# Spreading the rounding of weight blocks over the steps, and loading two inputs at once

## The chip, the cores and the metric

The kernel runs on one core of a Trainium2 chip. Its engines work side by side, each through its own queue of instructions: TensorE (PE in the profile) multiplies matrices, VectorE (DVE), ScalarE (ACT) and GpSimd (POOL) work elementwise, and SyncE (SP) issues transfers; ScalarE and GpSimd issue some too. The metric is the device time of one execution in microseconds (us), as the median of the runs; lower is better.

## The reference

A batch of 8 sequences of 3008 tokens with 256 channels is filtered in the frequency domain, and a two-layer network with SiLU between its layers follows, token by token:

```python
X = np.fft.rfft(x, axis=1)
Y = X * (filt_r + 1j * filt_i)[None]
y = np.fft.irfft(Y, n=3008, axis=1).reshape(24064, 256)
h = y @ w_in                     # 256 -> 2048
out = (h / (1 + np.exp(-h))) @ w_out   # 2048 -> 256
```

The weights w_in and w_out arrive as 64-bit numbers and are turned into 32-bit ones inside the kernel, on their bits.

## The kernel before, in words

**Two halves that overlap.** The Fourier part of a batch (`spectral(b)`) is a chain of small matmuls with fixed tables: `stage1` over blocks of rows, `forward`, a product with the filter, `inverse`, and `stage3`, which leaves the batch as y. The network part runs over pairs (batch, half, range of tokens), 48 of them, in steps: each pair takes 8 steps, and step jp of a pair uses the weights of hidden units 256 jp to 256 jp + 255. The first batch's Fourier part has nothing to run beside and comes first, with as much of the weights as fits; from then on the steps run without a break, and the Fourier part of the next batch is put between their matmuls.

**A step** is written as two generators. `hidden(step)` (lines 737 to 784) multiplies by the first layer with seven matmuls in place of eight (a Strassen-like scheme with combined weights), `project(step)` (line 796) multiplies the step before by the second layer, seven matmuls again. Each step has 8 rounds; in each round one piece of `hidden` is written, one piece of `project`, and then all pieces that were put there by `put(step, round, piece)` and are due. The order in which the code writes them is the order in each engine's queue. In `hidden` the matmuls and sums, by the names used from here on, are:

- round 0: matmul A11 into the bank px; ScalarE copies it (first copy).
- round 1: matmul A12 into one half of the bank pyz; VectorE makes *sum 1* of it and the first copy; then the *late pair*, the two last differences of the step before (`finish`).
- round 2: matmul S2 on px; second copy; SiLU of sum 1.
- round 3: matmul S1 into the other half of pyz.
- round 4: matmul S3 on px; third copy; *sum 2* of S1 and the third copy.
- round 6: matmul A22 on px; SiLU straight from px, which frees it for the next A11; SiLU of sum 2.
- round 7: matmul S4 on the S1 half; *sum 3* of it and the second copy; SiLU of sum 3; then the *differences* of three results (one instruction of 512 columns).

The matmul S1 waits for sum 1 and A12 of the next step for sum 3. In steps 1 to 6 the second batch's `stage1` (two matmuls of 512 columns, line 335) comes after round 3.

**Weight blocks.** There are 16 blocks of 128 hidden units, j = 0 to 15. Step jp of a pair needs blocks 2 jp and 2 jp + 1. A block is loaded (`weights`), split into exponent and mantissa (`split`: two VectorE instructions at lines 945 and 947, then two on ScalarE at 952 and 953), rounded (`rounded`: three VectorE instructions at 965, 967, 971), and put in its places (`placed`: two at 980). For each pair of blocks four combinations follow (`combine_weights`, line 721 of the helper `combine`), in one go or in two halves. Blocks 0 to 8 are done before the steps begin, blocks 9 to 15 inside steps 0 to 6 by the `put` calls at lines 1170 to 1182, each split, rounded (and, for the first three, with the four combinations of an earlier pair between) in round 1 and placed in round 5.

**The time before the steps.** The second batch's first two inputs are loaded by GpSimd's queue (line 1115) into the two halves of `x_all`, which the first batch used until its last first-stage matmul; two pairs of `stage1` matmuls of the second batch (line 1143) read them. Their results are stored to DRAM by GpSimd (`store_rows`), behind a small copy into `gate` (line 1151) that makes the stores wait for a block to be placed. Dummy matmuls (`idle_wide`, line 1154) fill TensorE's wait for the last transposed data of the first batch; then come four `stage3` and the steps.

Of the kernel before, what the change touches and what calls it, by code (L numbers as in the profile page):

```python
# [58 lines left out]
NJ = DFF // 128  # L59
# [8 lines left out]
A11, A12, S3, A22, S1, S2, S4 = range(7)  # L68
ROUNDS = 8
# [101 lines left out]
def kernel(  # L171
# [9 lines left out]
    nc = tc.nc  # L181
# [46 lines left out]
    w_t = cpool.tile([128, NJP, 7, 2, 128], FP32)  # L228
    warm = cpool.tile([128, 1], FP32)
    bias_t = cpool.tile([128, 5], FP32)  # L230
    gate = cpool.tile([128, 1], FP32)
    x_all = xpool.tile([128, 2, 2, 2 * C], FP32)
    x_t = [x_all[:, i] for i in range(2)]
# [34 lines left out]
    def spectral(b):  # L268
# [4 lines left out]
        xs, us, t2s, banks, prods, halves, t4s = {}, {}, {}, {}, {}, {}, {}  # L273
# [33 lines left out]
        def load_x(u, queue=None):  # L307
# [6 lines left out]
            for h in range(2):  # L314
                for r0, nr in ((0, 32), (32, N1 - 32)):
# [3 lines left out]
                                    offset=x.offset + (b * S + 32 * r0 + 4 * u + 2 * h) * C,  # L319
                                    ap=[[32 * C, nr], [32 * N1 * C, 2], [1, 2 * C]]))  # L320

        def sums(u):
            ut = x_t[0] if u == 7 else upool.tile([128, 2, 512], FP32, name=f"u_{b}_{u}", tag="u")
            xt = xs.pop(u)
            for par, op in ((0, ALU.add), (1, ALU.subtract)):
                nc.vector.tensor_tensor(out=ut[0:111, par], in0=xt[0:111, 0], in1=xt[0:111, 1], op=op)
            us[u] = ut
# [268 lines left out]
        def evict_y(g, h):  # L596
# [2 lines left out]
            copy = nc.scalar.copy if h else nc.vector.tensor_copy  # L599
            copy(out=dst[:, :, h, :, n0:n0 + 4], in_=us["pd", g][h].rearrange("p a i n -> p a n i"))  # L600

        return dict(us=us, store_rows=store_rows, evict_y=evict_y, evict_t1=evict_t1, halves=halves, load_first=load_first, stage1_first=stage1_first, load_x=load_x, sums=sums, stage1=stage1, reverse_x=reverse_x,
                    load_fold=load_fold, fold=fold, stage1_fold=stage1_fold, evict_fold=evict_fold,
                    load_t2=load_t2, forward=forward, multiply=multiply, add=add, inverse=inverse, inverse_first=inverse_first, rows_first=rows_first, even=even, rows=rows, load_t4=load_t4, load_t4_rows=load_t4_rows, stage3=stage3)

# [5 lines left out]
    def put(step, rnd, piece, *args):  # L611

        pending.append((step + rnd / ROUNDS, len(pending), lambda: piece(*args)))
# [103 lines left out]
    v, gp = nc.vector, nc.gpsimd  # L717
    ty, g_t, acc, unfinished = {}, {}, {}, []

    def combine(eng, out, in0, in1, op):  # L720
        eng.tensor_tensor(out=out, in0=in0, in1=in1, op=op)  # L721
# [176 lines left out]
    def load_weights(j, queue=None):  # L898

        if j in (8, 11, 12, 13):  # L900
            pool, tag = (t4pool, "t4") if j in (11, 12) else (upool, "u")
            raw = pool.tile([128, 2, 512], U32, name=f"raw_{j}", tag=tag)
        else:

            if j in (0, 2):
                t = ypool.tile([128, 2, HALF], FP32, name=f"raw_{j}", tag="y")
                raws.setdefault("tiles", []).append(t)
                raws["at"] = t.rearrange("p a n -> p (a n)").bitcast(U32)[:, 0:2048]
                raws["y"] = raws["at"]
                raws.setdefault("first", raws["at"])  # L910
            elif j == 4:
                raws["at"] = spool.tile([128, 2048], U32, name=f"raw_{j}", tag="s")
            elif j == 6:
                raws["at"] = gpool.tile([128, 2048], U32, name=f"raw_{j}", tag="g")
            elif j in (9, 14):
                raws["at"] = raws["y"]
            at = 1024 * (j in (1, 3, 5, 7, 10, 15))
            raw = raws["at"][:, at:at + 1024].rearrange("p (w n) -> p w n", w=2)
        queue = queue or nc.sync
        queue.dma_start(  # L920
            out=raw[:, 0].rearrange("p (a n) -> p a n", a=2),
            in_=moe_w_in.bitcast(U32)[:, 256 * j:256 * j + 256].rearrange("(a p) n -> p a n", p=128))
        queue.dma_start(out=raw[:, 1], in_=moe_w_out.bitcast(U32)[128 * j:128 * j + 128, :])
        raws[j] = raw
# [37 lines left out]
    def round_weights(*js):  # L962
        for j in js:
            lo, hi, e, m, ef, mf, mo, _, _ = raws[j]
            v.scalar_tensor_tensor(out=mo, in0=lo, scalar=2.0 ** -52, in1=mf, op0=ALU.mult, op1=ALU.add)
            if j not in (0, 2, 6):
                v.tensor_scalar(out=e, in0=ef, scalar1=255.0, scalar2=float(1 << 23),
                                op0=ALU.min, op1=ALU.mult)
        for j in js[::-1]:
            hi, e, eo = raws[j][1], raws[j][2], raws[j][8]  # L970
            v.scalar_tensor_tensor(out=eo, in0=hi, scalar=0x80000000, in1=e,
                                   op0=ALU.bitwise_and, op1=ALU.bitwise_or)

    def place_weights(*js, eng=None):
        for j in js:
            mo, eo = raws.pop(j)[6:8]
            for w in range(2):
                cols = slice(256 * w, 256 * w + 256)
                dst = places(j, w) if w == 0 else places(j, w).rearrange("p k (q i) -> p k q i", q=4)
                (eng or v).tensor_tensor(out=dst, in0=columns(mo[:, cols], w), in1=columns(eo[:, cols], w),  # L980
                                         op=ALU.mult)

    def load_exact(j):
        for k in range(2):
            nc.sync.dma_start(out=places(j, 0)[:, k],
                              in_=moe_w_in[128 * k:128 * k + 128, 128 * j:128 * j + 128])
            nc.sync.dma_start(out=places(j, 1)[:, k].rearrange("p (q i) -> p q i", q=4),
                              in_=columns(moe_w_out[128 * j:128 * j + 128, :], 1)[:, k])

    def combine_weights(jp, part=None, eng=None):  # L990

        eng = eng or v

        def w(c):
            return w_t[:, jp, c]
        if part != 1:
            combine(eng, w(S1), w(S3), w(A22), ALU.add)
            combine(eng, w(S2), w(S1), w(A11), ALU.subtract)
        if part != 0:
            combine(eng, w(S3), w(A11), w(S3), ALU.subtract)  # L1000
            combine(eng, w(S4), w(A12), w(S2), ALU.subtract)

    def weights(*js, queue=None):
        for j in js:
            if wide:
                load_weights(j, queue)

    def bits(*js):
        if wide:
            bits_of_weights(*js)  # L1010

    def converted(*js):
        if wide:
            convert_weights(*js)

    def split(*js):
        bits(*js)
        converted(*js)

    def rounded(*js):  # L1020
        if wide:
            round_weights(*js)

    def placed(*js, eng=None):
        if wide:
            place_weights(*js, eng=eng)
        else:
            for j in js:
                load_exact(j)
# [15 lines left out]
    def idle_wide(n, ps=None, rhs=None):  # L1045

        ps = ps or bank(0, "idle")
        for _ in range(n):
            nc.tensor.matmul(out=ps[:, 0], lhsT=wx_t, rhs=wide_rows if rhs is None else rhs,
                             start=True, stop=True)  # L1050
# [3 lines left out]

    by_gpsimd = (0, 1, 2, 3, 4)
    part, second = spectral(0), spectral(1)
    weights(0, 1, 2, 3)
    place = part["load_first"]()
# [35 lines left out]
    for k in range(16):  # L1094
        part["stage1_first"](k, 1)
        if k < 12:
            part["stage1_first"](k + 4, 0)
    weights(6, 7)
    part["forward"](0, fill=4)
    placed(0, 1)  # L1100
# [3 lines left out]
    def products(g):  # L1104
        for k in range(2):
            part["multiply"](g, k)
            if g in by_gpsimd:
                part["add"](g, k)
# [2 lines left out]
        part["inverse_first"](g)  # L1111
        part["rows_first"](g)

    for u in range(2):
        second["load_x"](u, nc.gpsimd)
    products(0)
    products(1)
    inverse(0)
# [26 lines left out]
    placed(4, 5)  # L1145
    rounded(6, 7)
    placed(6, 7)
    split(8)
    rounded(8)
    placed(8)  # L1150
    gp.tensor_copy(out=gate, in_=w_t[:, 4, A11, 0, 0:1])
    for u in range(2):
        second["store_rows"](u)
    idle_wide(14)
    for g in range(4):
        part["stage3"](g)
    nc.sync.dma_start(out=wi_t, in_=wi_dram.ap())
    second["load_x"](2)
    weights(10, 11, 12)
    second["load_x"](3)  # L1160
    weights(13)
    early[0] = None
    plan_rest(0, part)
    for g in (4, 5):
# [2 lines left out]
        put(20, 0, lambda t=t, dram=dram: nc.sync.dma_start(out=t, in_=dram.ap()))  # L1167
    for b in range(1, B):
        plan(b, second if b == 1 else spectral(b))
    for j in range(9, NJ):  # L1170
        if j < 12:
            put(j - 9, 1, lambda j=j: (split(j), combine_weights(j - 8), rounded(j)))
        else:
            put(j - 9, 1, lambda j=j: (split(j), rounded(j)))
        put(j - 9, 5, placed, j)
        if j % 2:

            put(*((j - 8, 5) if j < 15 else (j - 9, 6)), combine_weights, j // 2, 0)
            put(*{13: (j - 8, 7), 15: (j - 8, 1)}.get(j, (j - 7, 5)), combine_weights, j // 2, 1)

        if j < 11:
            put(j - 9, 1, weights, j + 5)

    per = len(PAIRS) * 2

# [4 lines left out]
    for pair in range(len(pairs)):  # L1190
        step, rnd = combines[pair % per] if pair != 1 else (7, 5)
        pending.append((pair // per * STEPS + step + rnd / ROUNDS, 98, lambda pair=pair: tokens(pair)))
        for chunk in range(2 if pair < len(pairs) - 1 else 0):
            step, rnd = stores[pair % per][chunk]
# [56 lines left out]
```

## Time and profile before

| what | value |
|---|---|
| median of 3 runs | 2580.62 us (2579.96 to 2583.24) |
| profiled execution, its own time | 2580.55 us |
| its span in the profile | 2578.7 us |
| TensorE busy | 2555.9 us, 99% |
| VectorE, ScalarE, GpSimd busy | 65%, 42%, 16% |
| dummy matmuls before stage 3 | 62.5 to 68.7 us |
| stage 3 of the first batch | 71.3 to 78.1 us |
| first matmul (A11) of steps 0 to 4 | 78.87, 86.65, 95.48, 103.60, 111.71 us |
| first matmul of steps 5 to 8 | 119.69, 127.54, 136.19, 142.56 us |

All times in the views are microseconds from the start of the span. A row of the timeline gives start, duration, engine, line of the code, operation, and destination and source with their shapes; in brackets stands how long the engine was idle before it and what it waited for. A duration can be longer than the distance to the next start, since an engine takes up the next instruction before the last one has ended. A row of the table of stretches gives the busy time of TensorE, its weight loads, VectorE, ScalarE and GpSimd in that stretch, with the number of instructions, then the granted TensorE clock as a share of full speed, the mean busy share of the transfer engines and GB/s. In the page's row PEclk each digit stands for a fortieth of the span.

### The profile page before, as it was taken

The numbers are of one execution on the slowest core, as the hardware profiler recorded it, in microseconds if no ns is written. First come the engines' busy times: TensorE is split into PE (matmuls) and PEld (weight loads), VectorE is DVE, ScalarE is ACT, GpSimd is POOL, SyncE is SP. The second block draws the span as 40 slices with busy tenths as digits, with TensorE's granted clock in tenths as the row PEclk, the third lists the DMA queues.
The fourth block names the chain that finished last, engine by engine and source line by source line (L and its number), as shares of the span: only waits on it lengthen the run. The fifth ranks groups of instructions, "written<-read, shape, count | busy, mean of one in ns | idle before, by whom it ended". The sixth has DMA issues, their size and how long they took to land.

```text
span 2578.7 us, 48117 instructions
## 1 busy us (share of the span) xinstructions
PE 2555.9 (99%) x18852; PEld 2196.2 (85%) x18852; DVE 1665.8 (65%) x3588; ACT 1086.0 (42%) x3010; POOL 421.3 (16%) x670
## 2 busy tenths in 40 slices
PE   8999999999999999999999999999999999999998
PEld 6788888888888888888888888988888888888987
DVE  7866666666666666666666666666666666555554
ACT  3544444444444444434444434444444444444443
POOL 2211111121112111311122111211121112101101
PEclk9899999999999999999999999999999999999999
DMA  8621232222222222222223222331232311210011
GB/s 277 171 62 50 71 79 63 60 64 75 60 63 69 70 62 58 76 73 64 64 59 88 51 66 58 80 80 46 66 79 65 74 42 28 64 19 16 9 17 16
DMA packets 200443, 171.08 MB, mean 66 GB/s; under 512 B 122100, under 2 KB 174180, under 8 KB 199428
## 3 DMA queue, kind: packets, MB, share of 16 engines
q1 hardware_dynamic: 179000, 117.32, 19.8%
q0 software_dynamic: 16992, 44.91, 5.5%
q10 hardware_dynamic: 4224, 5.77, 0.8%
q8 instruction: 148, 2.42, 0.4%
q14 instruction: 79, 0.65, 0.1%
HBM read 96.07 MB, written 81.26 MB: 69 GB/s over the span
## 4 chain that ended last, share of the span: by engine, by line
PE 97%; DVE 1%; DMA 1%; ACT 0%; issue 0%; SPq 0%; DVEq 0%; ACTq 0%
PE acc L813 44%; PE px L750 26%; PE pyz L750 19%; PE pd L580 3%; PE pb L457 2%; PE pc L500 2%; PE pf L424 1%; PE pc L522 0%; PE pa L344 0%; PE pa L335 0%; DMA d<-q 0%; DMA t<-d 0%; DMA raw<-in_moe_w_in_dram 0%; DVE g L721 0%; DVE w_t L721 0%
## 5 line engine op out<-in xcount | busy, mean ns | idle before, releaser
L813 PE MATMUL acc<-g,w_t 128*128 128x256 f32 (+1 forms) x5376 | 1509.2, 375 | 0.4 <-DVE g L721 0.4
L813 PEld LDWEIGHTS acc<-g,w_t 128*128 128x128 f32 x5376 | 1021.6, 190 | 115.8 <-DVE g L721 0.8
L721 DVE TENSOR_TENSOR g<-pyz,abc 128x256 f32<-128x256 f32 (+1 forms) x1152 | 479.9, 417 | 620.3 <-ACT abc L771 356.0
L721 DVE TENSOR_TENSOR g<-g 128x256 f32<-128x256 f32 (+3 forms) x1152 | 599.4, 520 | 196.7 <-ACT g L754 183.6
L750 PE MATMUL px<-ty,w_t 128*128 128x256 f32 (+1 forms) x2304 | 678.3, 376 | 1.4 <-ACT abc L765 1.0
L754 ACT ACTIVATE g<-g 128x256 f32<-128x256 f32 (+1 forms) x1152 | 472.9, 411 | 250.9 <-DVE g L721 250.9
L750 PEld LDWEIGHTS px<-ty,w_t 128*128 128x128 f32 x2304 | 432.3, 190 | 64.9 <-issue 6.2
L721 POOL TENSOR_TENSOR s<-s 128x256 f32<-128x256 f32 (+1 forms) x329 | 254.8, 792 | 1416.6 <-DVE s L833 1350.6
L750 PE MATMUL pyz<-y,w_t 128*128 128x256 f32 (+1 forms) x1536 | 454.3, 378 | 0.4 <-DVE g L721 0.4
L750 PEld LDWEIGHTS pyz<-y,w_t 128*128 128x128 f32 x1536 | 283.9, 190 | 48.2 <-DVE g L721 7.9
L765 ACT COPY abc<-px 128x256 f32<-128x256 f32 (+1 forms) x384 | 141.3, 368 | 372.8 <-PE px L750 372.8
L771 ACT COPY abc<-px 128x256 f32<-128x256 f32 (+1 forms) x384 | 141.5, 368 | 338.1 <-PE px L750 337.1
L754 ACT ACTIVATE g<-px 128x256 f32<-128x256 f32 (+1 forms) x384 | 145.8, 380 | 300.2 <-PE px L750 300.1
L750 PE MATMUL px<-y,w_t 128*128 128x256 f32 (+1 forms) x768 | 232.7, 385 | 0.8 <-DVE y L594 0.8
L750 PE MATMUL pyz<-ty,w_t 128*128 128x256 f32 (+1 forms) x768 | 225.4, 375 | 0.2 <-DVE g L721 0.2
L750 PEld LDWEIGHTS px<-y,w_t 128*128 128x128 f32 x768 | 140.6, 190 | 32.9 <-DVE y L600 5.8
L750 PEld LDWEIGHTS pyz<-ty,w_t 128*128 128x128 f32 x768 | 144.6, 190 | 18.7 <-DVE g L721 1.0
L758 ACT COPY abc<-px 128x256 f32<-128x256 f32 (+1 forms) x384 | 135.3, 352 | 53.7 <-PE px L750 53.6
L580 PEld LDWEIGHTS pd<-wi_t,t 48*64 48x64 f32 x3840 | 61.3, 135 | 26.2 <-ACT g L754 16.4
L436 POOL DMA_DIRECT2D d<-tf x144 | 71.4, 503 | 30.7 <-DVE tf L432 26.7
L863 DVE STREAM_TRANSPOSE o<-s 128x256 f32<-128x256 f32 x192 | 73.9, 423 | 1.5 <-issue 0.7
L833 ACT COPY s<-acc 128x512 f32<-128x512 f32 (+1 forms) x94 | 54.2, 577 | 47.6 <-PE acc L813 47.5
(137 smaller groups left out, 1262.4 us busy)
## 6 DMA issues: line engine op xcount, KB each, us to landing
t<-d SPq DMA_DIRECT2D x120, 192.0 KB
t<-d SPq DMA_DIRECT2D x84, 256.0 KB
d<-q POOLq DMA_DIRECT2D x84, 256.0 KB, 2.6
out_dram<-o SPq DMA_DIRECT2D x636, 32.0 KB
d<-tf POOLq DMA_DIRECT2D x144, 96.0 KB, 3.3
xr<-in_x_dram SPq DMA_DIRECT2D x6, 1472.0 KB
x_all<-in_x_dram SPq DMA_DIRECT2D x72, 96.0 KB
x_all<-xr SPq DMA_DIRECT2D x72, 96.0 KB
```

What stands on the lines that cost most here:

```text
L436: nc.gpsimd.dma_start(out=d1[k // 2, :, k % 2, n0:n0 + 4], in_=us["tf"][32 * k:32 * k + NS].rearrange("p q n c -> p (q n) c"))
L457: nc.tensor.matmul(out=ps[k][32 * j:32 * j + 32, ri, :], lhsT=d_t[rows, 4 * g + at, ri, :], rhs=rhs, start=True, stop=True)
L580: nc.tensor.matmul(out=ps[h][c0:c0 + 64, cb, i, :], lhsT=t4[rows, i, 128 * cb + c0:128 * cb + c0 + 64], rhs=wi_t[rows, :], start=True, sto ...
L721: eng.tensor_tensor(out=out, in0=in0, in1=in1, op=op)
L750: nc.tensor.matmul(out=out, lhsT=w_t[:, jp, c, 0], rhs=rhs, start=start, stop=True, skip_group_check=True)
L754: nc.scalar.activation(out=g[:, k, 0:n], in_=g[:, k, 0:n] if src is None else src, func=AFT.Silu)
L758: nc.scalar.copy(out=sums[:, 0, 0:n], in_=xo)
L765: nc.scalar.copy(out=sums[:, 1, 0:n], in_=xo)
L771: nc.scalar.copy(out=sums[:, 2, 0:n], in_=xo)
L813: nc.tensor.matmul(out=acc[pair][i][:, h, 0:n], lhsT=w_t[:, jp, c, 1], rhs=g[:, k, 0:n], start=(jp == 0 and h == 0), stop=last, skip_group ...
L833: copy(out=s[:, 2 * i:2 * i + 2, 0:n], in_=acc[pair][i][:, :, 0:n])
L863: v.transpose(out=o[:, :, h, :], in_=results[pair][:, ((2, 6), (4, 1))[chunk][h], :])
```

## The change

The two loads of the second batch's inputs on GpSimd become one on SP, in pieces of 8 KB per row, written between the loads of blocks 5 and 6. Block 8 is no longer split, rounded and placed before the steps: it takes step 0, round 1, and the blocks after it follow at about seven rounds from each other, with the rounding one round after the splitting from block 11 on. The combinations and the loads of blocks 13 to 15 move with them. The gate reads a place of block 6 in place of one of block 8, and there are 16 dummy matmuls instead of 14.

```diff
+        def load_two():
+            load_rows(x_all.rearrange("p i a n -> p (i a n)"), 0, 2)
+            for u in range(2):
+                xs[u] = x_t[u].rearrange("p a n -> p (a n)")
...
+    second["load_two"]()
     weights(6, 7)
...
-    for u in range(2):
-        second["load_x"](u, nc.gpsimd)
     products(0)
...
-    split(8)
-    rounded(8)
-    placed(8)
-    gp.tensor_copy(out=gate, in_=w_t[:, 4, A11, 0, 0:1])
+    gp.tensor_copy(out=gate, in_=w_t[:, 3, A11, 0, 0:1])
     for u in range(2):
         second["store_rows"](u)
-    idle_wide(14)
+    idle_wide(16)
...
     second["load_x"](3)
-    weights(13)
...
-    for j in range(9, NJ):
-        if j < 12:
-            put(j - 9, 1, lambda j=j: (split(j), combine_weights(j - 8), rounded(j)))
-        else:
-            put(j - 9, 1, lambda j=j: (split(j), rounded(j)))
-        put(j - 9, 5, placed, j)
+    turns = {8: (0, 1), 9: (1, 0), 10: (1, 7), 11: (2, 6), 12: (3, 5), 13: (4, 4), 14: (5, 2), 15: (6, 0)}
+    for j, (step, rnd) in turns.items():
+        turn = step * ROUNDS + rnd
+        put(0, turn, split, j)
+        if j < 11:
+            put(0, turn, combine_weights, j - 7)
+        put(0, turn + (j > 10), rounded, j)
+        put(0, turn + 4, placed, j)
         if j % 2:
-            put(*((j - 8, 5) if j < 15 else (j - 9, 6)), combine_weights, j // 2, 0)
-            put(*{13: (j - 8, 7), 15: (j - 8, 1)}.get(j, (j - 7, 5)), combine_weights, j // 2, 1)
-        if j < 11:
-            put(j - 9, 1, weights, j + 5)
+            put(0, turn + 4, combine_weights, j // 2, 0)
+            put(0, turn + 6, combine_weights, j // 2, 1)
+        if j in (8, 9, 10):
+            put(0, turn + 4, weights, j + 5)
```

More of the change, by code (lines that the diff above doesn't have):

```diff
@@ L600, in evict_y @@
             copy(out=dst[:, :, h, :, n0:n0 + 4], in_=us["pd", g][h].rearrange("p a i n -> p a n i"))
-        return dict(us=us, store_rows=store_rows, evict_y=evict_y, evict_t1=evict_t1, halves=halves, load_first=load_first, stage1_first=stage1_first, load_x=load_x, sums=sums, stage1=stage1, reverse_x=reverse_x,
+        return dict(us=us, store_rows=store_rows, evict_y=evict_y, evict_t1=evict_t1, halves=halves, load_first=load_first, stage1_first=stage1_first, load_x=load_x, load_two=load_two, sums=sums, stage1=stage1, reverse_x=reverse_x,
                     load_fold=load_fold, fold=fold, stage1_fold=stage1_fold, evict_fold=evict_fold,
```

## The prediction

> **What bounds the kernel now.** The page comes first: TensorE is busy for 99% of the span, so time can only be won or lost where it waits or runs at half clock.
>
> ```profile
> span 2578.7 us, 48117 instructions
> PE 2555.9 (99%) x18852; PEld 2196.2 (85%) x18852; DVE 1665.8 (65%) x3588; ACT 1086.0 (42%) x3010; POOL 421.3 (16%) x670
> PEclk9899999999999999999999999999999999999999
> ```
>
> From 142.56 us (the first matmul of step 8) to 2350 us TensorE is busy for 2206.2 of 2207.4 us. All that the change touches lies before that point, and whatever is won or lost there moves the end one for one. The stretches of that beginning, with the granted clock as the third figure from the end:
>
> ```profile
> 66.00:70.00 4.00, 2.69 (x13) 2.03 (x11) 3.97 (x9) 1.98 (x5) 0.00 (x0) 1.00 0.62 153
> 70.00:72.00 2.00, 0.96 (x39) 0.89 (x43) 1.58 (x5) 0.00 (x0) 0.00 (x0) 0.93 1.04 285
> 72.00:74.00 2.00, 2.00 (x88) 2.00 (x83) 0.76 (x2) 0.72 (x2) 0.00 (x0) 0.50 0.63 225
> 82.00:84.00 2.00, 1.05 (x4) 0.30 (x2) 1.97 (x6) 1.63 (x4) 0.00 (x0) 1.00 0.96 309
> 86.00:88.00 2.00, 2.00 (x6) 1.55 (x6) 0.87 (x3) 0.65 (x3) 0.00 (x0) 0.50 1.06 378
> ```
>
> The dummy matmuls end at 68.7, the first batch's stage 3 starts at 71.3 when its last load has landed, and it runs at half clock until 78.1; a second spell at half clock follows at 85.3 to 88.7. Then come the steps. The timeline of VectorE in step 2 to 3 (start, duration, operation) shows where a weight block fits:
>
> ```profile
> 105.02 0.69 DVE L721 TENSOR_TENSOR g<-g 128x512 f32<-128x512 f32 x1 [0.48 <-ACT g L754]
> 105.63 0.42 DVE L721 TENSOR_TENSOR g<-pyz,abc 128x256 f32<-128x256 f32 x1
> 105.96 0.87 DVE L721 TENSOR_TENSOR g<-g 128x256 f32<-128x256 f32 x2
> 106.76 0.42 DVE L945 TENSOR_SCALAR e<-raw 128x512 uint32<-128x512 uint32 x1
> 107.09 0.42 DVE L947 TENSOR_SCALAR m<-raw 128x512 uint32<-128x512 uint32 x1
> 108.48 0.69 DVE L965 SCALAR_TENSOR_TENSOR m<-raw,m 128x512 f32<-128x512 uint32 x1 [0.97 <-ACT m L953]
> 109.09 0.42 DVE L967 TENSOR_SCALAR e<-e 128x512 uint32<-128x512 f32 x1
> 109.55 0.69 DVE L971 SCALAR_TENSOR_TENSOR e<-raw,e 128x512 uint32<-128x512 uint32 x1
> 110.29 0.42 DVE L721 TENSOR_TENSOR g<-pyz,abc 128x256 f32<-128x256 f32 x1
> ```
>
> The differences, sum 1 and the late pair follow at once (105.02 to 106.76); then VectorE has 3.5 us until sum 2 at 110.29, and splitting and rounding a block fills exactly this hole. TensorE's S1 matmul, by contrast, follows sum 1 closely:
>
> ```profile
> 106.42 0.59 PE L750 MATMUL pyz<-ty,w_t 128*128 128x256 f32 x2
> ...
> 130.58 0.70 PE L750 MATMUL pyz<-ty,w_t 128*128 128x256 f32 x2 [0.19 <-DVE g L721]
> ```
>
> Sum 1 started at 105.63 and is done at 106.05; S1 may start some 0.05 later and does at 106.42. The slack is 0.3 us. At 130.58, where a combination stood ahead of sum 1, it was already gone.
>
> [...] the spells last from 71.7 to 81.9 (three windows) and 85.3 to 88.7 (one). [...] S1 writes the other half of the bank that sum 1 reads, and it waits all the same (130.58).
>
> **The change, part by part.** Edits that I cost at nothing:
> - The load of the second batch's inputs: two POOL issues (0.54 and 0.75 us, landing after 8.2) become one of SP of the same 768 KB, behind block 5's weights (about 41 us). It needs TensorE's last first-stage matmul (32.7) and serves matmuls at 58.95; landing within even 9 us leaves 9 spare. POOL idles 2.48 us there anyway. Queued behind it are blocks 6 and 7, issued 41.3 to 46.4 before; they need at most about 2 us more and are read first at 59.78. If that cover were gone, every us would count.
> - Block 8 leaves the time before the steps: VectorE 72.82 to 77.1 and ScalarE 1.24 us, all under stage 3's matmuls (71.33 to 78.11). The last copy of stage 3 starts 0.06 after its matmul, so there is nothing to win.
> - The gate reads block 6 instead: POOL's eight stores move from 77.4 to about 71. The last stage-3 load lands at 71.3, and the stores' reader runs at 137.7. SP's loads of blocks 13 to 15 move later by up to a step and a half, and still come three steps or more ahead of use.
> - In step 0, block 8 does what block 9 did in the same place: the same instructions, 0.
> - Two more dummies: four passes of 0.22 us, ending at 69.6 and not 68.7, before the first stage-3 matmul (70.25). Cost 0, or 0.9 if the load came earlier. The gain lies between 0 and 2.5: 64 stage-3 matmuls take 1.08 us at full clock at 158.3 in the chain, 256 take 4.3 and not 6.8. Whether a gap shrunk from 2.6 to 1.7 us keeps the clock can't be read from this trace: a window with three matmuls in it (81.9 to 85.3) was followed by half clock, one about four fifths full (37.6 to 41.0; 1.68 of 2.00 us from 38 to 40) was not. I take 0 and keep 2.5 for the range.
>
> What remains is the order in the steps. Slots from VectorE's rows (start to next start): split 0.67, four combinations 1.46, rounding 1.68, placing 0.67, half a combination 0.7 to 0.8. ScalarE's two conversions take 1.15. I walked the three queues in the code's new order with these slots, 0.432 us per matmul, 1.72 for a stage-1 pair. The same walk in the old order gives 63.7 us from step 0 to step 8, the trace 63.69. New waits of TensorE:
> - Block 9 stands at step 1, round 0: split, combinations and rounding, 3.81 us, now ahead of sum 1. The differences' slot ended at 88.41, so sum 1 starts at 92.2 and not 89.28, and S1, which ran at 90.31, at 92.7: **2.4**. Its placing and combinations (2.2) come before sum 3, which the next A12 waits for: 0.7.
> - Block 10 (step 1, round 7) is again ahead of sum 1. S1 came 2.84 us after A11 (95.48, 98.32), the differences' slot ended at +2.04; 2.04 + 3.81 + 0.47 = 6.3 is 3.5 late. ScalarE's conversions also stand ahead of the first copy; the walk gives **3.7**.
> - Block 11: rounding ahead of sum 1 of step 3, **1.7**.
> - Block 12 (step 3, round 5): the conversions stand ahead of the SiLU that frees the px bank, 1.6, and sum 3 behind the rounding and its wait makes A12 late, 1.0: **2.6**.
> - Block 13: the same, 0.8 and 1.0, and placing and half a combination ahead of sum 1, 1.2: **3.0**.
> - Blocks 14 and 15: 0.55 and 0.9.
>
> Together 15.5. The present waits go: steps 2 to 6 take 40.71 us (from A11 to A11) where 5 x (14 x 0.432 + 1.72) is 38.8, step 7 0.3 too many: 2.2. Net **+13.3**. Stalls of 2 us and more leave windows half empty, and each spell at half clock costs half of 3.4, 1.7 us. None to three may follow; I take one or two, **+2.6**. After step 8 TensorE has nothing to catch up with.
>
> Sum: 2580.55 (the profiled execution's own time, 0.07 under the median) + 13.3 + 2.6 = 2596.4, **2596**.
>
> **The rivals.**
> - *Clock kept.* The dummies hold the clock through stage 3 and no stall costs it later: 2580.55 + 13.3 - 2.5 = 2591. For it: the gap shrinks by a third. Against: stage 3's own small matmuls did not raise the clock in two windows.
> - *Not slower.* Spacing the blocks really removes waits: rounding one round after splitting hides the 0.97 us, so the 2.2 us of present waits and stage 3's 2.5 go, 2576. It needs the 3.8 us of a block to fit between the differences and sum 1; the place has 0.3 us, so it decides only if S1 did not wait for sum 1, and 130.58 shows that it does.
> - *Transfers late.* Blocks 6 and 7 behind the 768 KB, or blocks 13 to 15 behind SP's x loads, arrive after VectorE asks: another 5 us or more, 2602 and up. DMA was just 54% busy from 50 to 54, which speaks against.
> - *No effect.* The new places do change VectorE's order, so only cancelling could give it.
>
> **How the numbers follow.** The likeliest case 0.74, clock kept 0.14, late transfers 0.05, not slower or no effect 0.07. The range 2588 to 2602 holds the first two with 3 us for errors of the walk. A measurement here tells 0.2% (5.2 us) from no change; the likeliest case and the first and third rivals lie above. Of the not-slower case, its 4 to 5 us are mostly inside 0.2%: faster 0.02, same 0.05, slower 0.93.
>
> **What would show it.** Right: S1 of steps 1 and 2 waiting for VectorE for 2 us and more; a SiLU released late at blocks 12 and 13; step lengths near 11, 12, 11, 10, 10.5, 8 and 6.7 for steps 1 to 7, where they are 8.8, 8.1, 8.1, 8.0, 7.9, 8.7, 6.4; A11 of step 8 near 156 to 160. Wrong: step lengths as before, a DMA named in front of VectorE's rows at 59.8, or a stage 3 of under 5 us with step 8 before 142.

## The result

| | before | after |
|---|---|---|
| median | 2580.55 us of 4 runs (2579.96 to 2583.24) | 2596.66 us of 4 runs (2595.00 to 2597.97) |
| profiled execution, its own time and span | 2580.55, 2578.7 us | 2597.8, 2595.9 us |
| TensorE busy | 2555.9 us | 2561.7 us |
| first matmul of step 0, of step 8 | 78.87, 142.56 us | 78.33, 158.33 us |

The changed kernel is slower by 16 us: ratio 1.0060, 95% interval 1.0043 to 1.0077. The lines of the page of the changed kernel that answer to those shown of before:

```profile
span 2595.9 us, 48120 instructions
PE 2561.7 (99%) x18856; PEld 2199.5 (85%) x18856; DVE 1664.8 (64%) x3588; ACT 1087.6 (42%) x3010; POOL 420.7 (16%) x668
PEclk9899999999999999999999999999999999999999
```

The engines did the same work, but for the two more dummies on TensorE. TensorE's idle time, span less busy time, went from 22.8 to 34.2 us, and its busy time grew by 5.8 us: 0.9 ahead of step 0, which are the dummies, and 4.8 in the steps. Where it happened is seen in one row for each kernel, the stretch from the first matmul of step 0 to that of step 8 (columns as in the prediction: length, then busy time of TensorE, weight loads, VectorE, ScalarE and GpSimd, granted clock, DMA share, GB/s). After, and then before:

```profile
78.33:158.33 80.00, 66.53 (x235) 46.31 (x235) 55.73 (x134) 35.22 (x83) 12.09 (x24) 0.91 0.43 121
```

```profile
78.87:142.56 63.69, 61.68 (x235) 44.95 (x236) 52.39 (x127) 32.35 (x81) 14.31 (x30) 0.95 0.57 161
```

The same 235 matmuls took 16.3 us longer. TensorE's idle time went from 2.01 to 13.47 us, which is 11.5 of it; its busy time went from 61.68 to 66.53, which is the other 4.8. So the loss is two things: waits, and the half clock that followed some of them.

Busy time doesn't part the two cleanly, because a wait lengthens it as well. In four rows of TensorE around the wait of step 1:

```profile
89.04 0.60 PE L756 MATMUL px<-ty,w_t 128*128 128x256 f32 x2
89.47 0.59 PE L819 MATMUL acc<-g,w_t 128*128 128x256 f32 x2
91.69 0.70 PE L756 MATMUL pyz<-ty,w_t 128*128 128x256 f32 x2 [1.62 <-DVE g L727]
92.22 0.59 PE L819 MATMUL acc<-g,w_t 128*128 128x256 f32 x2
```

Without a wait the next pair follows after 0.43 us, though the row before is 0.60 long. A row ahead of a wait counts with its whole length (0.59 in place of 0.43), and behind the wait the next pair follows after 0.53: a wait costs some 0.26 us more than the idle time noted with it, and these count as busy. A second count goes by the clock records. TensorE worked at half clock for 6.26 us of this stretch before and for 12.95 after. At half clock a pair follows after 0.85 or 0.86 us (85.65 to 86.50 to 87.36 in the changed kernel), so about half of that time is lost: 3.1 and 6.5. By this count half clock is 3.3 of the 16.3 us, and waits are 13.0.

Step 0 began 0.54 us earlier than before. The other 1.4 us of the span lie behind step 8, where TensorE's pauses for nothing that the profile names grew from 1.0 to 2.1 us (the last section comes back to them).

Step by step, from A11 to A11:

| step | 0 | 1 | 2 | 3 | 4 | 5 | 6 | 7 |
|---|---|---|---|---|---|---|---|---|
| before | 7.78 | 8.83 | 8.12 | 8.11 | 7.98 | 7.85 | 8.65 | 6.37 |
| foretold | as before | 11 | 12 | 11 | 10 | 10.5 | 8 | 6.7 |
| after | 7.32 | 11.31 | 14.94 | 11.04 | 9.71 | 10.69 | 8.13 | 6.86 |

The timeline of VectorE in the changed kernel, in step 2 (block 10), shows the cause:

```profile
98.96 0.69 DVE L727 TENSOR_TENSOR g<-g 128x512 f32<-128x512 f32 x1 [0.48 <-ACT g L760]
99.57 0.42 DVE L951 TENSOR_SCALAR e<-raw 128x512 uint32<-128x512 uint32 x1
99.90 0.42 DVE L953 TENSOR_SCALAR m<-raw 128x512 uint32<-128x512 uint32 x1
100.24 1.55 DVE L727 TENSOR_TENSOR w_t<-w_t 128x256 f32<-128x256 f32 x4
101.70 0.69 DVE L971 SCALAR_TENSOR_TENSOR m<-raw,m 128x512 f32<-128x512 uint32 x1
102.31 0.42 DVE L973 TENSOR_SCALAR e<-e 128x512 uint32<-128x512 f32 x1
102.76 0.69 DVE L977 SCALAR_TENSOR_TENSOR e<-raw,e 128x512 uint32<-128x512 uint32 x1
103.37 0.42 DVE L727 TENSOR_TENSOR g<-pyz,abc 128x256 f32<-128x256 f32 x1
103.70 0.87 DVE L727 TENSOR_TENSOR g<-g 128x256 f32<-128x256 f32 x2
```

Between the differences (98.96) and sum 1 (103.37) stand the split, four combinations and the rounding: 3.80 us from 99.57 to 103.37, the 3.81 that the prediction added up. Before, sum 1 followed the differences at once. The later of its two inputs here, the first copy, was done at 101.52 (101.17 and 0.35, below), and sum 1 still started 1.85 us later, behind the rounding: VectorE took its work in the order of the code. ScalarE, in the same step, and two more rows of TensorE and one of step 4:

```profile
100.02 0.72 ACT L958 ACTIVATE e<-e,bias_t 128x512 f32<-128x512 uint32 x1 [1.10 <-DVE e L951]
100.65 0.61 ACT L959 ACTIVATE m<-m 128x512 f32<-128x512 uint32 x1
101.17 0.35 ACT L764 COPY abc<-px 128x256 f32<-128x256 f32 x1
...
101.57 0.70 PE L756 MATMUL px<-ty,w_t 128*128 128x256 f32 x2 [1.91 <-ACT abc L764]
...
103.84 1.22 PE L756 MATMUL pyz<-ty,w_t 128*128 128x256 f32 x2 [1.14 <-DVE g L727]
...
122.94 0.70 PE L756 MATMUL px<-y,w_t 128*128 128x256 f32 x2 [1.36 <-ACT g L760]
```

S1 of step 1 (91.69, above) waits 1.62 us for sum 1 behind block 9. In step 2 S2 waits 1.91 for the first copy, which stands behind block 10's conversions on ScalarE (100.02 to 101.17), and S1 another 1.14 for sum 1. A11 of step 4 waits 1.36 for the SiLU behind block 12's conversions. The clock behind the stall of step 2 is seen in four stretches of 3.41 us. They are cut along the clock records: from 30 to 165 us of this kernel each stretch of one clock is a whole multiple of 3.413 us long, with half clock from 68.5 to 82.2, 85.6 to 89.0 and 102.7 to 109.5, which are 4, 1 and 2 of them. One such 3.413 us is called a window, here and in the prediction.

```profile
99.24:102.65 3.41, 1.50 (x6) 0.70 (x5) 3.38 (x9) 1.84 (x4) 0.00 (x0) 1.00 0.21 82
102.65:106.06 3.41, 2.27 (x6) 1.85 (x6) 2.53 (x7) 0.45 (x2) 0.00 (x0) 0.50 0.01 2
106.06:109.48 3.42, 3.42 (x5) 1.35 (x4) 0.00 (x0) 0.70 (x2) 0.00 (x0) 0.50 0.00 0
109.48:112.89 3.41, 3.41 (x17) 2.97 (x16) 1.56 (x4) 2.49 (x6) 1.97 (x4) 1.00 0.68 181
```

TensorE was busy for 1.50 of the first 3.41 us, and the next window ran at half clock. That one was 2.27 us busy, and half clock was kept for another. So 6.8 us at half clock followed one stall of about 3 us (1.91 and 1.14), and step 2 is 2.9 us longer than foretold. TensorE worked for 5.68 of the 6.8 us, half of which is 2.8.

### The profile page after: what moved, and what is told of

Its sections match the earlier page's. It is cut to its first block, busy times and chain, and to the rows that moved or that the text cites. A ratio compares the mean times of both kernels' runs of the same rounds, so it can differ in the third digit from the quotient of the medians.

```text
span 2595.9 us, 48120 instructions
## 1 busy us (share of the span) xinstructions
PE 2561.7 (99%) x18856; PEld 2199.5 (85%) x18856; DVE 1664.8 (64%) x3588; ACT 1087.6 (42%) x3010; POOL 420.7 (16%) x668
## 3 DMA queue, kind: packets, MB, share of 16 engines
q8 instruction: 148, 2.42, 0.4%
## 4 chain that ended last, share of the span: by engine, by line
PE 95%; DMA 2%; DVE 2%; ACT 1%; issue 0%; SPq 0%; ACTq 0%; DVEq 0%
PE acc L819 43%; PE px L756 25%; PE pyz L756 19%; PE pd L586 3%; PE pb L463 2%; PE pc L506 2%; PE pf L430 1%; DMA filt<-in_filt_r_dram 1%; PE pa L350 0%; DMA w_t<-in_x_dram 0%; PE pa L341 0%; DMA x_all<-in_x_dram 0%; DMA d<-q 0%; DVE w_t L727 0%; DMA raw<-in_moe_w_in_dram 0%
## 5 line engine op out<-in xcount | busy, mean ns | idle before, releaser
L756 PEld LDWEIGHTS pyz<-y,w_t 128*128 128x128 f32 x1536 | 284.0, 190 | 50.6 <-DVE g L727 10.5
```

The source lines that it names most:

```text
L756: nc.tensor.matmul(out=out, lhsT=w_t[:, jp, c, 0], rhs=rhs, start=start, stop=True, skip_group_check=True)
```

## The experiments

Each ratio below is against the kernel before, run beside it on the same chip; the median of before in those sessions was 2578.89 to 2579.53 us.

**One: which half of the change.** The change has a front (the load, the dummies, the transfers) and the turns of the blocks. Two kernels take one half each. The first is the changed kernel with the old turns:

```diff
+    split(8)
+    rounded(8)
+    placed(8)
+    gp.tensor_copy(out=gate, in_=w_t[:, 4, A11, 0, 0:1])
...
     second["load_x"](3)
+    weights(13)
...
-    turns = {8: (0, 1), 9: (1, 0), 10: (1, 7), 11: (2, 6), 12: (3, 5), 13: (4, 4), 14: (5, 2), 15: (6, 0)}
...
+    for j in range(9, NJ):
...
```

The second is its counterpart, the kernel before with these same lines the other way round (new turns, gate on block 6, block 13 loaded inside the steps).

> The changed kernel's front (one load of SP for the second batch's first two inputs, 16 dummies) with the old order of the blocks: block 8 before the steps, blocks 9 to 15 in the hole behind the late pair. Theory (the new turns carry the whole loss): steps 1 to 7 are 8 to 9 us long again, no wait of S1 over 0.5 us, and the time is 2579 to 2581, at most 0.5 to 1 us under before, because step 0 began 0.54 us earlier in the changed kernel. Rival (the load and the moved transfers cost the time): 2590 or more. Rival (the old front kept the clock better): a loss of 2 to 5 us, seen before step 0.

> The counterpart: the old front (two loads issued by GpSimd, 14 dummies) with the new turns of blocks 8 to 15 and the gate on block 6. Theory: the step lengths of the changed kernel return (near 7, 11, 12 to 15, 11, 10, 10.5, 8, 7) and the time is 2594 to 2598. Rival (front): 2580 to 2584.

Measured: the new front with the old turns has a median of 2578.01 us, ratio 0.9996 (0.9988 to 1.0004). Its steps 1 to 7 are 8.15, 8.13, 8.12, 7.98, 7.85, 8.65 and 6.37 us, and no wait of S1 in them is over 0.2. The old front with the new turns has 2596.64, ratio 1.0072 (1.0060 to 1.0085), and steps 1 to 7 of 11.32, 15.00, 11.04, 9.72, 10.69, 8.14 and 6.85: the changed kernel's, within 0.06. The turns carry the whole loss, the front none.

**Two: the place of blocks 9 and 10.** Two rounds were changed, so that both blocks stand behind the late pair.

```diff
-    turns = {8: (0, 1), 9: (1, 0), 10: (1, 7), ...
+    turns = {8: (0, 1), 9: (1, 1), 10: (2, 1), ...
```

> The changed kernel with block 9 one round later (step 1, round 1) and block 10 two rounds later (step 2, round 1), so that both stand behind sum 1 and the late pair. Theory: step 1 falls from 11.3 to near 7.8 and step 2 from 14.9 to near 9; 6 us are won of the queue alone and up to 3 more if the half-clock spell of step 2 goes with its stall: 2588 to 2591. Rival (only the clock matters): step 1 stays above 10, 2593 to 2594. Rival (the loss belongs to the blocks' number of operations, not to their place): no change, 2596 to 2597.

Measured: 2586.29 us, ratio 1.0026 (1.0015 to 1.0037); 10.4 us less than the changed kernel, and less by as much than the old front with the new turns (2596.64), which ran in the same session. That is a larger gain than expected. Steps 1 and 2 fell to 7.80 and 9.03. VectorE's timeline in step 1 of this kernel, with the hole used:

```profile
82.86 0.69 DVE L727 TENSOR_TENSOR g<-g 128x512 f32<-128x512 f32 x1 [0.48 <-ACT g L760]
83.47 0.42 DVE L727 TENSOR_TENSOR g<-pyz,abc 128x256 f32<-128x256 f32 x1
83.80 0.88 DVE L727 TENSOR_TENSOR g<-g 128x256 f32<-128x256 f32 x2
84.59 0.42 DVE L951 TENSOR_SCALAR e<-raw 128x512 uint32<-128x512 uint32 x1
```

Sum 1 (83.47) follows the differences at once, and the same work comes behind the late pair. The stretch of this kernel that answers to the two rows in the section on the result is

```profile
75.12:145.44 70.32, 60.89 (x235) 42.67 (x236) 55.38 (x134) 34.31 (x83) 12.29 (x24) 1.00 0.50 137
```

No half clock at all. The 60.89 us are still not the matmuls' own time: in the second kernel of experiment four, which has the old turns, this stretch (82.13 to 143.75) is at full clock too, and TensorE is busy for 59.12 of its 61.62 us. Steps 1 and 2 are 9.4 us shorter than in the changed kernel, step 3 is 0.4 longer. The queue alone was to give 6 of them, which leaves some 3 for half clock, the upper end of what was expected for it; in the changed kernel TensorE worked for 9.05 us of these two steps at half clock, worth 4.5 at most. Part of that is not the blocks' doing. In this execution stage 3 ran at full clock from 72.0 us on, step 0 began 3.2 us earlier, and the spell at 85.6, which the kernel before has as well (85.4), is absent. That differs from run to run, and the medians say 10.4 us in all.

**Three: what in the place costs.** Two kernels with two small moves each, in different steps; each was run once, so the step lengths are the evidence, and the time is only a check. Block 9's rounding and block 12's conversions later:

```diff
-        put(0, turn, split, j)
+        put(0, turn, *((bits, j) if j == 12 else (split, j)))
+        if j == 12:
+            put(0, turn + 1, converted, j)
...
-        put(0, turn + (j > 10), rounded, j)
+        put(0, turn + (j > 10 or j == 9), rounded, j)
```

Block 12's conversions as above, its rounding later too, and block 9's combinations:

```diff
-            put(0, turn, combine_weights, j - 7)
+            put(0, turn + (j == 9), combine_weights, j - 7)
...
-        put(0, turn + (j > 10), rounded, j)
+        put(0, turn + (4 if j == 12 else j > 10), rounded, j)
```

> The changed kernel with two small moves in different steps. First, block 9's rounding stands one round later, behind sum 1 and the late pair; its split and the four combinations stay ahead. Theory (S1 is late by the slots that stand ahead of sum 1): step 1 falls from 11.31 by the 1.68 us of the rounding, to 9.6 to 9.7. Second, block 12's two conversions stand one round later on ScalarE, behind the SiLU that frees the px bank, with the rounding still one round behind the split. Theory: A11 of step 4 is not late any more (step 3 from 11.04 to 9.4 or 9.5), but the rounding then waits longer for the conversions ahead of sum 3, so the same time comes back in step 4 (from 9.71 to 11.2 or 11.4): that move alone wins nothing. In all 1.6 to 1.7 us less, near 2595. Rival (what counts is how much work a step holds, not where it stands): step lengths within 0.3 us of the changed kernel's.

> The changed kernel with two other moves. Block 9's four combinations alone go one round later, behind sum 1; the rounding stays ahead of it. ScalarE's conversions end about 1.0 us behind the split, so the rounding waits for them and only part of the combinations' 1.46 us can be won: step 1 from 11.31 to 10.8. Second, block 12's conversions stand one round later, as in the other run, but its rounding goes three rounds further, behind the late pair of step 4. Theory: step 3 falls from 11.04 to 9.4 or 9.5 and step 4 from 9.71 to near 8.9. In all 2.9 us less, near 2594. Rival (only one of the two waits is real): step 3 or step 4 as in the changed kernel.

| step | 1 | 2 | 3 | 4 |
|---|---|---|---|---|
| changed kernel | 11.31 | 14.94 | 11.04 | 9.71 |
| rounding of 9 later, conversions of 12 later | 9.65 | 14.69 | 9.51 | 11.25 |
| combinations of 9 later, conversions and rounding of 12 later | 12.56 | 12.73 | 9.51 | 8.82 |

The first kernel did in steps 1, 3 and 4 what was expected. The rounding's 1.66 us left step 1 when it left the place ahead of sum 1. The clock isn't the reason, though this step met less half clock here (1.2 us, to 85.8, and not 3.4): S1 still waited 1.02 us for sum 1, so VectorE set its time in both kernels. Block 12's conversions, moved behind the SiLU, gave 1.53 us to step 3 and took 1.54 in step 4, because the rounding now waited for them ahead of sum 3. The timeline of TensorE in that kernel shows the wait in its new place, at A12 of step 4, where the changed kernel had 0.72:

```profile
121.87 0.70 PE L756 MATMUL pyz<-y,w_t 128*128 128x256 f32 x2 [2.36 <-DVE g L727]
```

In the second kernel, with the rounding out of that place too, steps 3 and 4 are 9.51 and 8.82: both waits are real, and both go when conversions and rounding leave. Step 1 missed: 12.56 and not 10.8. The clock records show half clock from 93.2 to 96.6 us, behind the stall of this step. (The changed kernel's spell lay at 85.6 to 89.0, ahead of the stall, and TensorE then waited less.) The timeline parts the two: S1 started 5.59 us after A11 and not 6.04, so the combinations did give 0.45 of the 0.5 expected; and from S1 to the next A11, which holds the spell, passed 6.97 us and not 5.27. By that the spell cost 1.7 us, half of its 3.4. The times were 2593.80 and 2594.05 us (expected near 2595 and 2594).

**Four: the front.** The new load had brought a gain that I had not foreseen: the second batch's first-stage matmuls started at 55.56 us, where they had started at 58.95. (It isn't the same in every execution: six of the eight kernels with the new load behind the table start them at 54.8 to 55.6, the other two at 58.8 and 59.4, without a wait for the table; the three with the old front start at 56.5 to 59.0.) Two kernels ask why, both with the old turns. In the first the load stays on SP, but ahead of the weights of blocks 4 and 5:

```diff
-    weights(4, 5)
...
     second["load_two"]()
-    weights(6, 7)
+    weights(4, 5, 6, 7)
```

In the second it is on ScalarE's queue, ahead of the last pieces of the two tables:

```diff
-    nc.scalar.dma_start(out=d_t[:, 16:NS], in_=d_dram[:, 16:NS])
-    nc.scalar.dma_start(out=e_t[:, 2:NG], in_=e_dram[:, 2:NG])
...
-    second["load_two"]()
+    second["load_two"](nc.scalar)
+    nc.scalar.dma_start(out=d_t[:, 16:NS], in_=d_dram[:, 16:NS])
+    nc.scalar.dma_start(out=e_t[:, 2:NG], in_=e_dram[:, 2:NG])
```

> The old order of the blocks with the one load of SP, as in the first run, but the load is issued ahead of the weights of blocks 4 and 5 and so ahead of the last pieces of the two tables that ScalarE's queue fetches (as the GpSimd loads were in the kernel before). If the place in the order of transfers is what gained 3 us at the second batch's first-stage matmuls: TensorE is idle again for 2 to 3 us near 41 to 45, these matmuls start at 57.5 to 59 instead of 54.9, and step 0 starts at 78 to 79. If the engine that issues, or the 8 KB pieces, gained it: 54.8 to 55.6 as with the later load. The time is 2578 to 2581 in either case.

> The old order of the blocks and 16 dummies, with the same single load in 8 KB pieces, but issued on ScalarE's queue just ahead of the last pieces of the two tables, so that it is certain to stand ahead of them. If the place ahead of the table of the second stage's factors is what cost the kernel before its idle time: TensorE waits 2 to 3 us for that table near 41 to 44 again and the second batch's first-stage matmuls start at 57 to 59. If GpSimd's issue, or the 4 KB pieces of its two loads, cost it: no such wait, and a start near 54.8 to 55.6.

The first told nothing of this: SP issued the load at 36.03 us, still behind the issue of table d_t (35.36), so the order that I wanted to undo was not undone; the matmuls started at 54.82 and the time was 2578.06, ratio 0.9998 (0.9990 to 1.0007). The second forced the order. TensorE's timeline in it:

```profile
46.46 2.08 PE L463 MATMUL pb<-w_t,d_t 64*32 64x256 f32 x32 [5.90 <-DMA d_t<-d_tbl]
```

It waits 5.90 us for table d_t, and the first-stage matmuls start at 62.12. In the kernel with the old front and the new turns, where GpSimd issued the loads at 32.85 and ScalarE d_t at 35.61, the same wait bears the same name:

```profile
43.48 1.35 PE L457 MATMUL pb<-w_t,d_t 64*32 64x256 f32 x32 [2.00 <-DMA d_t<-d_tbl]
```

In before it was 3.01 us, put down to a VectorE instruction that ended at 44.51; the table's last piece had landed at 44.50. The trace's records of landings give the time from the issue of d_t to its last piece:

| | d_t issued | landed | between |
|---|---|---|---|
| before (768 KB ahead) | 36.20 | 44.50 | 8.30 |
| old front, new turns (ahead) | 35.61 | 43.34 | 7.73 |
| load ahead of the tables (ahead) | 37.87 | 46.33 | 8.46 |
| load ahead of blocks 4 and 5 (behind) | 35.36 | 40.78 | 5.42 |
| after (behind) | 35.97 | 40.07 | 4.10 |

Of all twelve kernels, the four with the load ahead have 7.7 to 8.7 us, the eight with it behind 4.1 to 5.4. So it is the place in the order of transfers: 768 KB that nobody needed before 55 us stood ahead of a table needed at 41.6. GpSimd's issue and the smaller pieces are not needed for it, since a single load in 8 KB pieces issued by ScalarE brought the wait back. That it was 5.90 and not 2 to 3 has other reasons: against before, d_t was issued 1.7 us later and TensorE was ready for it 1.1 us earlier (40.56, not 41.63). The time of the one run was 2582.81.

**Five: the clock of stage 3.** More dummies, so that they end when stage 3 begins; in the kernel before, and as the version meant to beat both (new load, old turns).

```diff
-    idle_wide(14)
+    idle_wide(20)
```

> The kernel before with 20 dummies and not 14, which at 0.44 us a dummy end near 71.3 instead of 68.7, when stage 3's main part starts. If the idle time between dummies and stage 3 sets stage 3's half clock: its 256 matmuls take near 4.3 us and not 6.8, and the time is 2578, 2 to 2.5 us under before. If the small matmuls of stage 3 lower the clock by themselves: 6.8 us as before and 2580.5 to 2581.

> The version meant to beat both: the one load of SP in its new place, the old order of the blocks, and 20 dummies, so that these end near 67.3, when stage 3's main part starts. If the idle time ahead of stage 3 sets its clock: stage 3 starts at full clock and ends 0.6 to 2 us earlier than with 16 dummies, bounded by the gap of about 1.5 us that TensorE had in its stream of small matmuls at full clock; 2575.5 to 2577.5. If the clock doesn't depend on it: 2578, as with 16.

TensorE's timeline in the kernel before with 20 dummies:

```profile
61.40 8.80 PE L1049 MATMUL idle<-d_t,wx_t 96*128 96x256 f32 x40
70.12 3.69 PE L580 MATMUL pd<-wi_t,w_t 48*64 48x47 f32 x220
75.33 0.79 PE L580 MATMUL pd<-wi_t,w_t 48*64 48x47 f32 x36 [1.52 <-issue]
```

Stage 3 now runs at full clock: 220 matmuls in 3.69 us, where half clock took 6.78 for 254. Then TensorE stops for 1.52 us, waiting for nothing that the profile names, and step 0 met a half-clock spell instead. Median 2579.05, ratio 1.0000 (0.9992 to 1.0009): no gain. With the new load stage 3 runs at full clock too and stops for 1.33 us; the time is 2578.27, ratio 0.9992 (0.9983 to 1.0000), at the edge of what can be told, the same as with 16 dummies (2578.01) and above the 2575.5 to 2577.5 expected. Whether any of these is a real microsecond faster than before stays open.

**Six: the best turns with block 8 in the steps.** The walk of the three queues was asked for the places that lose least.

```diff
-    turns = {..., 9: (1, 0), 10: (1, 7), 11: (2, 6), 12: (3, 5), 13: (4, 4), 14: (5, 2), 15: (6, 0)}
+    turns = {..., 9: (1, 1), 10: (2, 1), 11: (3, 1), 12: (4, 2), 13: (4, 5), 14: (5, 2), 15: (6, 1)}
...
-        put(0, turn + (j > 10), rounded, j)
+        put(0, turn + (rnd > 1), rounded, j)
```

> The changed kernel with its blocks at the best places that the walk of the three queues finds while block 8 stays inside the steps: blocks 8 to 11 in the hole behind the late pair (round 1 of steps 0 to 3), blocks 12 to 15 at step 4 round 2, step 4 round 5, step 5 round 2 and step 6 round 1. Theory: steps 1 to 7 are 7.8, 9.1, 7.8, 9.6, 9.7, 7.8 and 6.6 us without half clock, 11 us less than the changed kernel's 76.0 in the walk and 3 us more than the old order's 62; with the half-clock spell of step 2 gone too: 2581 to 2585. Rival (block 8 inside the steps costs a whole block's worth wherever it stands, 4 us and more): 2587 to 2590.

Measured: 2580.76 us, ratio 1.0008 (0.9999 to 1.0017). Steps 1 to 7 are 8.82, 8.93, 7.80, 9.56, 10.02, 7.80 and 6.72. Only step 1 (a spell at 82.2 to 85.6) and step 5 are more than 0.2 off the walk. Its median is 15.9 us under the changed kernel's, with all of the change's other edits left in; the 2581 to 2585 expected were just missed, on the better side. What it still loses against the old turns sits mostly in steps 4 and 5, which hold three blocks, 12 to 14 (9.56 and 10.02 us, against 7.98 and 7.85).

## Why the prediction was right

The forecast was 2596, with 2588 to 2602; measured 2596.66. Its steps:

- *The load at nothing.* Right in the time (0.9996, 0.9988 to 1.0004), wrong in the reasoning. It asked if the new load lands in time, and not what the old one had kept waiting. Of the 3.4 us that the first-stage matmuls gained, 2.0 reached the start of stage 3 (69.35, not 71.33), and 0.5 the start of step 0, because stage 3, with a pause of 0.76 in it, took 8.24 us and not 6.78. The kernel before also had a half-clock spell from 44.4 to 47.8, behind its wait for the table, which the prediction didn't list and the changed kernel doesn't have.
- *Block 8's leaving, the gate, step 0.* Right: there was nothing to win under stage 3 (with block 8 back in its place there, in the new front with the old turns, the 254 matmuls ran in 7.07 us without a wait), and the stores, now from 67.6 us, kept nobody waiting.
- *Two more dummies, 0 taken.* Right, and for a simpler reason than argued: since all ahead of them came earlier, they ended at 66.2 and stage 3 began at 69.35, a gap of 3.2 us and not 1.7. The bound of 2.5 for a kept clock was too high: at full clock stage 3 takes 6.0 us (70.12 to 76.12), not 4.3, because of the 1.52 us pause.
- *Block 9, 2.4 + 0.7.* Measured 1.62 and 0.54, since TensorE ran at half clock until 89.0 and came to S1 later; the step is 11.31, foretold 11. The sign on record that S1 of steps 1 and 2 would wait 2 us and more did not come (1.62 and 1.14). In step 1 the half clock hid a part: the second kernel of experiment three, at full clock up to S1 and with less work ahead of sum 1, waited 2.84 there.
- *Block 10, 3.7.* 1.91 for S2 and 1.14 for S1, with a half-clock spell within; 14.94, foretold 12. This is the one step length that is clearly off, by the clock: half of 5.68 us is 2.8.
- *Blocks 11 to 15.* Measured 1.34 (1.7), 1.36 + 0.72 (2.6), 0.69 + 0.73 + 1.10 (3.0), 0.16 (0.55), 0.54 (0.9): each in its place and a sixth or more smaller than foretold, while the step lengths agree within 0.3. The idle time leaves out some 0.26 us a wait, as shown above; with it, blocks 11 and 12 are at 1.6 and 2.6.
- *The sums.* Waits +13.3 and clock +2.6 were foretold. By idle and busy time they measured +11.5 and +4.8. The prediction counted a wait as all time lost against 0.432 us a matmul, though, and the count by clock records is the nearer one: waits +13.0, clock +3.3. So the waits were sized well and the clock somewhat low: 6.7 us more at half clock are two windows' worth, where one or two were taken. The two aren't independent: a wait that comes behind a half-clock spell is shorter by what the spell has already cost, as at block 9 (1.62 us, and 2.84 in the kernel at full clock). Together 15.9 against 16.3.
- *What was luck.* The median within 0.7 us of the forecast. Runs of the changed kernel alone are 3 us apart, the earlier start of step 0 (0.5) and the pauses behind step 8 (1.4 more) weren't in the sum, and the walk's agreement in the old order (63.7, the trace 63.69) shows less than it seems: 3.1 us of these 63.69 are half clock, and the same order at full clock took 61.62. The step lengths carry the account, not the total.
- *The rivals.* "Clock kept" fell: stage 3 ran at half clock. "Not slower" fell with the waits of S1. "Transfers late" fell: VectorE's rows, at 59.78 before and at 56.38 now, wait for no DMA, and the front alone costs nothing.

The views that carried it were the timeline of VectorE, which showed both the hole and its size, and one wait of S1 in the kernel before, which showed that sum 1 has no slack.

## What to carry to other kernels

Before side work is moved within an engine's queue, find in the timeline which of the queue's instructions another engine waits for and how much slack each has; here step 1 took 7.80 us with block 9 behind the late pair and 11.31 with it one round earlier, and even distances were no help. When a stall is priced, ask too how busy it leaves the 3.41 us window of the clock records that it falls in: of the 29 windows here that ran at full clock and were under 60% busy, 24 were followed by half clock. And a transfer that is early enough can still be too early, if it stands ahead of one that is needed sooner: table d_t took 7.7 to 8.7 us from issue to landing behind 768 KB, and 4.1 to 5.4 us ahead of them.

## What the runs showed of the hardware that I had not expected

**Half clock followed the less busy windows.** I laid the 3.413 us grid of the clock records over 30 to 165 us of the twelve profiled executions (before, after and ten experiments) and took TensorE's busy share of each window and the clock of the next:

```
clock of the window   busy share      next at half   next at full
full                  under 0.40      10             0
full                  0.40 to 0.60    14             5
full                  0.60 and more   0              381
half                  under 0.86      16             0
half                  0.86 and more   12             24
```

No window at full clock that was 60% busy or more was followed by half clock, and none under 40% was spared. The share isn't all that counts: of four windows that were 44% busy, three were followed by half clock and one was not. At half clock no window under 86% came back, and a full one didn't always: of the ten windows that stage 3's small matmuls, 48x64 with 47 columns, filled whole, eight stayed at half clock and two came back (68.57 in the kernel with blocks 9 and 10 in the hole, 76.42 in the second of experiment four). What decides there isn't known. The bounds were drawn after the fact, around these windows, and no run tests them. The window from 99.24 to 102.65 in the changed kernel has 1.9 us of idle time in it, in one wait of 1.91, and half clock followed. The grid lies differently in each execution (a window begins at 30.77 us in before, at 30.99 in the changed kernel, at 33.23 in the old front with the new turns), so the same stall may meet it differently. Runs of one kernel spread by 3 to 7 us here, and those with more of the clock granted are on average the faster ones (of the 27 of before in the first session, 15 were granted 0.997 or more and average 2578.5 us, the other 12 average 2579.9); that the grid's place is the reason isn't shown.

**Pauses of TensorE behind a packet of the instruction queue.** A pause in stage 3 for nothing that the profile names comes in five kernels, each time 220 to 229 matmuls in. The trace's DMA records have the instruction queue (q8 on the page, 148 packets, 2.42 MB, so 16 KB each) land one packet 1.28 to 1.39 us ahead of TensorE's going on:

| kernel | packet landed | TensorE went on | between |
|---|---|---|---|
| before, 20 dummies | 73.97 | 75.33 | 1.36 |
| new front, 20 dummies | 72.28 | 73.60 | 1.32 |
| blocks 9 and 10 in the hole | 72.33 | 73.72 | 1.39 |
| blocks in or near the hole | 73.72 | 75.00 | 1.28 |
| after | 75.12 | 76.50 | 1.38 |

The matmuls there take 17 ns each (3.69 us for 220), and the five pauses 0.24 to 1.52 us. It isn't stage 3 of the first batch alone: the twelve executions have 34 pauses of 0.15 us and more put to nothing, those behind step 8 and one of 2.06 us at 50.93 in the kernel of experiment six among them, and in each TensorE went on 1.2 to 1.6 us after a packet had landed, while packets come some 17 us apart on average. Most of the packets have no such pause behind them: of 148 each, two in before and four in the changed kernel. That the packet is the cause is read from the times alone; no run tested it.
